# A new instruction order, a warm-up without a gap and a last row stored in unequal parts, in a kernel of four layers on one core

## The chip, the cores and the metric

The kernel runs on one core of a Trainium2 chip. The core has five engines with a queue each: TensorE (PE: matrix products, transposes; its weight loads, PEld, run beside the products), VectorE (DVE), ScalarE (ACT), GpSimd (POOL) and SyncE (SP, which here only issues DMAs). They run side by side and wait for one another by semaphores; within one queue the order is fixed. The metric is the time of one execution on the device in microseconds (us); less is better.

## The reference

Four layers in a row act on one sequence of 2048 rows of 512 numbers (bfloat16), two kinds in turn:

```python
def _A_ref(q, k, v, shift_k, ssm_k, ssm_D):
    k_shift = sum of 4 shifted copies of k, each times a row of shift_k
    kv = k_shift * v
    y = causal convolution of kv with ssm_k along the sequence (by FFT), per column
    y = y + kv * ssm_D
    return q * y

def _B_ref(x, w_gate, w_up, w_down):
    return (silu(x @ w_gate) * (x @ w_up)) @ w_down

x = A_q
x = x + _A_ref(_layernorm(x), A_k, A_v, A_shift_k, A_ssm_k, A_ssm_D)
x = x + _B_ref(_layernorm(x), B_w_gate, B_w_up, B_w_down)
x = x + _A_ref(_layernorm(x), A_k, A_v, A_shift_k, A_ssm_k, A_ssm_D)
x = x + _B_ref(_layernorm(x), B_w_gate, B_w_up, B_w_down)
```

The hidden width of B is 1792. The convolution in A has the same inputs both times and does not depend on x, so its result y is computed once and used in both A layers.

## The kernel before, in words

**The convolution.** The sequence is cut into four blocks of 512 rows. Each block of `kv` (by PE: "shift" products with diagonal matrices `dg`, then a DVE product with `vt`) and each block of the kernel `ssm_k` (called `hn`, turned by PE or DMA into `hs`) is brought into a spectrum by PE products with tables `fwd` of sines (made at the start on DVE and ACT). ACT copies the spectra out of PSUM (`ev`, `X`, `H`), DVE forms sums and differences (`G`, `m`), multiplies spectra (`t`, `Z`), and PE brings the result back with the table `inv` (`Yk`). This work is spread over the first two thirds of the run, beside the feed-forward units.

**The feed-forward units.** Each block of rows is worked in two halves of 256 rows, and in two layers, so there are 16 units. A unit's rows are normalised (DVE or ACT statistics; the power of -1/2 on GpSimd, `rstd`; the scaled rows `n` or `z`), multiplied with `Yk` and added to `xc`, normalised again and turned by a DMA on SP's queue into `zT` (the first unit's by PE). Then PE forms gate and up products in pairs of 128 hidden columns (`pf`, line 311), ACT evacuates them (silu into `sg`, line 970; copy into `ht`, line 974), DVE multiplies `ht` by `sg` (line 977), PE multiplies by the down weights (`pd`, line 990), ACT copies `pd` out (`dn`, line 1034), DVE adds it to the rows (line 1037), and for the second layer SP stores each row tile (line 1045).

**What sets the order.** Every instruction is first recorded with an engine, an assumed cost and its buffers (`add`). Then a written list, `ORDER`, gives each recorded step its place; the steps are put into the engines' queues in that sequence. `Plan.order` works out planned start times from the assumed costs, which decide which of the rotating buffers a tile takes. `Plan.issue` emits the steps, and where the plan leaves PE without work for over 0.5 us before 32 us it puts products of a constant tile in (`warm`, line 1264, called "warm-up products" here; PSUM tile `wm`); how many comes from the planned gap at 0.106 us each. In the kernel before they read a tile `wz` that DVE sets to 0.5.

**The opening.** SP loads `hn`, `kn` (keys), `vt`, `xc`, a second `hn`, `vt`, and the gate weights; two DMAs turn `fwd` into `inv`; then a key block and the other weights follow. ACT's queue loads the four taps (`tapR`) and one row (`drow`), then loads its function table and computes the sines. PE warms up, turns the taps (line 1133), transposes `hn` (line 477) and `kn` (line 366), and starts on the spectra (lines 311 and 458).

**The last row.** The very last unit ends with a row tile of 512 columns that is split into two parts of 256: DVE adds the first part from PSUM to the rows (line 1008) and SP stores it; PE itself adds the rows to the second part (line 949), ACT copies it out (line 1011) and stores it from its own queue (line 1014).

Of the kernel before, what the change touches and what calls it, by code (L numbers as in the profile page):

```python
# [9 lines left out]
P = 128  # L10
# [6 lines left out]
LN_EPS = 1e-5  # L17
# [33 lines left out]
LASTV = True  # L51
ORDER = [
# [186 lines left out]
def kernel(  # L239
# [1024 lines left out]
    def warm(ring, slot, n):  # L1264
        t = psp.tile([P, P], F32, name="wm", tag=f"{ring}{slot}")
        for _ in range(n):
            nc.tensor.matmul(t[:], lhsT=wz.t[:], rhs=wz.t[:], start=True, stop=True)  # L1267
# [33 lines left out]
```

## Time and profile before

| what | value |
|---|---|
| median of 3 runs | 344.79 us (344.21 to 345.18) |
| the profiled execution's own time | 344.93 us |
| its span, first to last instruction | 343.2 us |
| PE busy | 336.4 us (98%) |
| weight loads busy | 248.6 us (72%) |
| DVE busy | 283.4 us (83%) |
| ACT busy | 253.9 us (74%) |
| POOL busy | 35.3 us (10%) |
| gate and up products (line 311), 1792 | 110.4 + 110.2 us, 273 ns each as recorded |
| down products (line 990), 440 | 102.4 us |
| warm-up products, 31 | 3.6 us |
| power steps on GpSimd, 24 + 8 | 690 to 1790 ns each |

The recorded time of a product includes its way through the array and overlaps the next one; the distance between starts is shorter (64 gate and up products in 6.99 us, 109 ns each). Busy shares are therefore shares of time with something running, not of peak. Idle time of an engine that is not the bound costs nothing; the chain of waits tells which engine was the bound at each moment.

### The profile page before, as it was taken

How to read it: one execution, taken by the hardware profiler on the slowest of the kernel's cores; microseconds unless marked ns; L12 is line 12 of the kernel's file. 1: busy time of each engine (PE TensorE's matmuls, PEld its weight loads, DVE VectorE, ACT ScalarE, POOL GpSimd, SP SyncE). 2: the span in 40 equal slices, each digit the busy share in tenths (PEclk: the TensorE clock that was granted, in tenths of full speed). 3: DMA queues.
4: the chain of work that ended last, by engine and by line, in shares of the span. 5: the costliest groups of instructions: out<-in, count | busy, mean ns of one | idle time of the engine just before them, and what ended most of it. 6: DMA issues, size and time to landing. Idle time of an engine off the chain costs nothing.

```text
span 343.2 us, 6553 instructions
## 1 busy us (share of the span) xinstructions
PE 336.4 (98%) x2579; PEld 248.6 (72%) x2610; DVE 283.4 (83%) x482; ACT 253.9 (74%) x504; POOL 35.3 (10%) x46
## 2 busy tenths in 40 slices
PE   8999999999999999999999999999999999999996
PEld 7756868768687676858586777768685877777783
DVE  8899999899999999899999999989998433726022
ACT  6999999899997765958789995779475464446261
POOL 4010100203111000103110100201101001000000
PEclk9999999999999999999999999999999999999999
DMA  7999218310116044040101014210101100110101
GB/s 273 336 316 341 52 27 112 77 32 0 34 31 94 14 95 138 2 94 3 32 2 46 2 46 79 76 32 1 32 0 33 35 13 0 39 39 8 24 26 37
DMA packets 42088, 22.95 MB, mean 67 GB/s; under 512 B 33861, under 2 KB 39882, under 8 KB 42058
## 3 DMA queue, kind: packets, MB, share of 16 engines
q1 hardware_dynamic: 41904, 22.47, 26.6%
q8 instruction: 20, 0.33, 0.4%
q14 instruction: 10, 0.08, 0.1%
q10 hardware_dynamic: 154, 0.07, 0.1%
HBM read 12.33 MB, written 2.10 MB: 42 GB/s over the span
## 4 chain that ended last, share of the span: by engine, by line
PE 91%; ACT 4%; DVE 3%; issue 1%
PE pf L311 54%; PE pd L990 28%; PE ps L311 6%; PE ps L458 1%; ACT H L419 1%; PE wm L1267 1%; DVE bnst L809 1%; ACT hs L487 1%; PE pt L477 1%; ACT X L419 0%; ACT n L859 0%; PE pt L366 0%; DVE m L540 0%; DVE t L665 0%; DVE Z L667 0%
## 5 line engine op out<-in xcount | busy, mean ns | idle before, releaser
L311 PE MATMUL pf<-zT,wu_sb 128*128 128x256 bf16 x896 | 110.4, 273 | 0.1
L311 PE MATMUL pf<-zT,wg_sb 128*128 128x256 bf16 x896 | 110.2, 273 | 0.2
L990 PE MATMUL pd<-wd_sb,ht 128*128 128x512 bf16 (+1 forms) x440 | 102.4, 372 | 1.2
L311 PEld LDWEIGHTS <-wu_sb 128*128 128x128 bf16 x896 | 87.7, 98 | 16.4
L311 PEld LDWEIGHTS <-wg_sb 128*128 128x128 bf16 x896 | 87.6, 98 | 16.5 <-issue 0.8
L974 ACT CAST ht<-pf 128x512 bf16<-128x512 f32 x112 | 64.0, 591 | 29.3 <-PE pf L311 29.1
L970 ACT ACTIVATE sg<-pf 128x512 bf16<-128x512 f32 x112 | 65.5, 603 | 17.4 <-PE pf L311 15.1
L990 PEld LDWEIGHTS <-ht 128*128 128x128 bf16 x462 | 45.2, 98 | 42.5
L977 DVE TENSOR_TENSOR ht<-ht,sg 128x1024 bf16<-128x1024 bf16 (+1 forms) x64 | 39.0, 617 | 24.0 <-ACT sg L970 18.7
L814 POOL TENSOR_TENSOR rstd<-ve,nhalf 128x2 f32<-128x2 f32 x24 | 23.0, 958 | 217.8 <-DVE ve L812 207.6
L1034 ACT CAST dn<-pd 128x512 bf16<-128x512 f32 x30 | 17.0, 589 | 21.0 <-PE pd L990 20.9
L809 DVE BATCH_NORM_STATS2 bnst<-xc 128x6 f32<-128x512 bf16 x48 | 31.6, 684 | 0.6
L419 ACT ACTIVATE X<-ps 128x512 bf16<-128x512 f32 x32 | 19.2, 611 | 4.0 <-PE ps L311 3.4
L653 DVE TENSOR_TENSOR t<-X,G 128x2048 bf16<-128x2048 bf16 x18 | 21.9, 1218 | 0.1
L657 DVE TENSOR_TENSOR t<-X,G 128x2048 bf16<-128x2048 bf16 x18 | 21.9, 1216 | 0.0
L1037 DVE TENSOR_TENSOR xc<-xc,dn 128x1024 bf16<-128x1024 bf16 x15 | 10.3, 689 | 13.4 <-ACT dn L1034 13.2
L665 DVE TENSOR_TENSOR t<-t,t 128x2048 bf16<-128x2048 bf16 x12 | 14.7, 1222 | 0.3
L667 DVE TENSOR_TENSOR Z<-Z,t 128x2048 bf16<-128x2048 bf16 x12 | 14.6, 1220 | 0.2
L840 POOL TENSOR_TENSOR rstd<-ve,nhalf 128x2 f32<-128x2 f32 x8 | 8.7, 1088 | 59.2 <-ACT ve L838 59.1
L419 ACT ACTIVATE H<-ps 128x512 bf16<-128x512 f32 x24 | 13.8, 610 | 0.1
L886 DVE TENSOR_TENSOR n<-n,Yk 128x1024 bf16<-128x1024 bf16 x15 | 10.3, 688 | 4.1 <-ACT n L859 3.8
L604 ACT ACTIVATE kc<-kTb,tapF 128x512 bf16<-128x512 bf16 x16 | 12.1, 783 | 0.0
(105 smaller groups left out, 323.3 us busy)
## 6 DMA issues: line engine op xcount, KB each, us to landing
hn<-in_A_ssm_k_dram SPq DMA_DIRECT2D x4, 512.0 KB, 4.1
vt<-in_A_v_dram SPq DMA_DIRECT2D x4, 512.0 KB, 5.9
xc<-in_A_q_dram SPq DMA_DIRECT2D x4, 512.0 KB, 5.3
out_dram<-xc SPq DMA_DIRECT2D x15, 128.0 KB, 1.8
wg_sb<-in_B_w_gate_dram SPq DMA_DIRECT2D x1, 1792.0 KB
wu_sb<-in_B_w_up_dram SPq DMA_DIRECT2D x1, 1792.0 KB, 8.5
wd_sb<-in_B_w_down_dram SPq DMA_DIRECT2D x1, 1280.0 KB, 12.0
kn<-in_A_k_dram SPq DMA_DIRECT2D x1, 512.0 KB, 4.5
```

What stands on the lines that cost most here:

```text
L311: nc.tensor.matmul(o, lhsT=lhsT, rhs=rhs, start=(n == 0), stop=(n == len(terms) - 1))
L419: add("ACT", act(D), lambda: nc.scalar.activation(out=view(), in_=ps.t[:], func=ACT.Copy, scale=scale), r=[ps], w=[(buf, keys)], conv=conv)
L653: dve(n * D, lambda t1=t1, part=part: nc.vector.tensor_mul(out=t1.t[:], in0=x.t[:, sl, 0, :], in1=g.t[:, sl, part, :]), [(x, key(slots, (0 ...
L657: dve(n * D, lambda t2=t2, part=part: nc.vector.tensor_mul(out=t2.t[:], in0=x.t[:, sl, 1, :], in1=g.t[:, sl, 1 - part, :]), [(x, key(slots ...
L665: dve(n * D, lambda t1=t1, t2=t2, comb=comb: nc.vector.tensor_tensor(out=t1.t[:], in0=t1.t[:], in1=t2.t[:], op=comb), [t2], [t1], conv=conv)
L809: add("DVE", 0.6, lambda st=st, i=i: nc.vector.bn_stats(out=st.t[:], in_=xs[c].t[:, i, :]), r=[(xs[c], (i,))], w=[st])
L814: add("POOL", pw, lambda: nc.gpsimd.tensor_tensor(out=rstd.t[:], in0=ve.t[:], in1=nhalf.t[:].to_broadcast((P, n)), op=ALU.pow), r=[ve, nha ...
L970: add("ACT", act(D), lambda ps=ps, o=o, sg=sg: nc.scalar.activation(out=sg.t[:, o:o + 2, :], in_=ps.t[:], func=ACT.Silu), r=[ps], w=[(sg, ...
L974: add("ACT", act(D), lambda ps=ps, o=o, ht=ht: nc.scalar.copy(out=ht.t[:, o:o + 2, :], in_=ps.t[:]), r=[ps], w=[(ht, (o // 2,))], due=(uni ...
L977: dve(n * W, lambda sg=sg, ht=ht: nc.vector.tensor_mul(out=ht.t[:], in0=ht.t[:], in1=sg.t[:]), [sg], [ht], due=(unit, k / pairs, 0.0, "h"))
L990: nc.tensor.matmul((pds[o] if not cs.start else pds[HP]).t[:, cs], lhsT=ht.t[:, q, o * P:(o + 1) * P], rhs=wt["d"].t[:, ft, cs], start=(ft ...
L1034: add("ACT", act(D), lambda o=o: nc.scalar.copy(out=dn.t[:, o, :], in_=pds[o].t[:]), r=[pds[o]], w=[(dn, (o,))], due=(unit, 1.0, 3.0, "h"))
```

## The change

Five things change in the code.

1. The warm-up products read `ones`, a constant of the framework that GpSimd writes before the engines start on the program, and DVE's memset of `wz` is gone.
2. The count of warm-up products leaves out a margin of 0.3 us where the planned gap starts between 0 and 8 us. The program now has 25 and 8 of them ahead of and behind the tap products (22 and 5 before), and 16 at a later place in the opening (4 before).
3. The last row tile is split into 320 and 192 columns instead of 256 and 256, with assumed costs to match.
4. The list `ORDER` is replaced by another one. The steps are the same; their sequence differs on every engine, from the first microseconds to the end.
5. A switch `VE_D` is added that would move one small step of the statistics from ACT to DVE. It is off, so nothing changes by it.

```diff
@@ -49,65 +49,67 @@
 LASTV = True
+TAIL = 320
+VE_D = False
 ORDER = [
-    0, 8, 122, 2, 4, 5, 12, 9, 3, 6, 1, 31, 32, 33, 10, 14, 7, 11, 15, 16, 18, 21, 17, 20, 22, 23, 36, 30, 56, 73, 153, 24, 40, 25, 41, 34, 42, 38,
...
+    0, 37, 6, 3, 4, 17, 9, 7, 8, 1, 2, 15, 61, 12, 5, 10, 11, 13, 39, 19, 14, 20, 16, 21, 25, 40, 38, 62, 63, 101, 30, 43, 22, 55, 26, 42, 24, 46, 56,
...
@@ -222,7 +224,7 @@
                         if busy.get((ring, i), 0.0) <= t:
-                            n = int((start - max(t, 0.3) - 0.3) / 0.106)
+                            n = int((start - t - (0.0 if 0.0 < t < 8.0 else 0.3)) / 0.106)
                             if n > 0:
                                 warm(ring, i, n)
@@ -835,8 +837,12 @@
-        add("ACT", TINY, lambda: nc.scalar.activation(out=ve.t[:], in_=sm.t[:, n:2 * n], func=ACT.Identity, scale=1.0 / D, bias=eps.t[:]),
-            r=[(sm, range(n, 2 * n)), eps], w=[ve])
+        if VE_D:
...
+        else:
+            add("ACT", TINY, lambda: nc.scalar.activation(out=ve.t[:], in_=sm.t[:, n:2 * n], func=ACT.Identity, scale=1.0 / D, bias=eps.t[:]),
+                r=[(sm, range(n, 2 * n)), eps], w=[ve])
@@ -942,7 +948,7 @@
-                halves = (slice(0, D // 2), slice(D // 2, D)) if unit == LAST_UNIT and o == HP - 1 else (slice(0, D),)
+                halves = (slice(0, TAIL), slice(TAIL, D)) if unit == LAST_UNIT and o == HP - 1 else (slice(0, D),)
@@ -980,7 +986,7 @@
-                halves = (slice(0, D // 2), slice(D // 2, D))
+                halves = (slice(0, TAIL), slice(TAIL, D))
@@ -989,7 +995,7 @@
-                    add("PE", pe(n) if not last else pe(n, D // 2), go, r=[ht, (wt["d"], (0 if fts[0] == 0 else 1,))],
+                    add("PE", pe(n) if not last else pe(n, css[0].stop - css[0].start), go, r=[ht, (wt["d"], (0 if fts[0] == 0 else 1,))],
@@ -1002,13 +1008,13 @@
-            for half_, (eng, cs) in enumerate((("DVE", slice(0, D // 2)), ("ACT", slice(D // 2, D)))):
+            for half_, (eng, cs) in enumerate((("DVE", slice(0, TAIL)), ("ACT", slice(TAIL, D)))):
                 copy = nc.scalar.copy if eng == "ACT" else nc.vector.tensor_copy
                 if LASTV and not half_:
-                    add(eng, 0.35, lambda cs=cs: nc.vector.tensor_add(out=x.t[:, i, cs], in0=x.t[:, i, cs], in1=pds[o].t[:, cs]),
+                    add(eng, 0.42, lambda cs=cs: nc.vector.tensor_add(out=x.t[:, i, cs], in0=x.t[:, i, cs], in1=pds[o].t[:, cs]),
...
@@ -1046,8 +1052,7 @@
-    wz = whole("wz", [P, P])
-    add("DVE", 0.07, lambda: nc.vector.memset(wz.t[:], 0.5), w=[wz], due=-80)
+    ones = nc.const_aps.tensor(1.0, (P, P), BF16)
@@ -1264,7 +1269,7 @@
         for _ in range(n):
-            nc.tensor.matmul(t[:], lhsT=wz.t[:], rhs=wz.t[:], start=True, stop=True)
+            nc.tensor.matmul(t[:], lhsT=ones, rhs=ones, start=True, stop=True)
```

More of the change, by code (lines that the diff above doesn't have):

```diff
@@ L837, in ln_stats_act @@
         ve, rstd = new("ve", "ve", [P, n], F32), new("rs", "rstd", [P, n], F32)
-        add("ACT", TINY, lambda: nc.scalar.activation(out=ve.t[:], in_=sm.t[:, n:2 * n], func=ACT.Identity, scale=1.0 / D, bias=eps.t[:]),
-            r=[(sm, range(n, 2 * n)), eps], w=[ve])
+        if VE_D:
+            add("DVE", 0.08, lambda: nc.vector.tensor_scalar(out=ve.t[:], in0=sm.t[:, n:2 * n], scalar1=1.0 / D, scalar2=LN_EPS,
+                                                             op0=ALU.mult, op1=ALU.add), r=[(sm, range(n, 2 * n))], w=[ve])
+        else:
+            add("ACT", TINY, lambda: nc.scalar.activation(out=ve.t[:], in_=sm.t[:, n:2 * n], func=ACT.Identity, scale=1.0 / D, bias=eps.t[:]),
+                r=[(sm, range(n, 2 * n)), eps], w=[ve])
         add("POOL", PWA, lambda: nc.gpsimd.tensor_tensor(out=rstd.t[:], in0=ve.t[:], in1=nhalf.t[:].to_broadcast((P, n)),
@@ L1004, in ffn @@
                 due=(unit, 1.0, 20.0, None))
-            for half_, (eng, cs) in enumerate((("DVE", slice(0, D // 2)), ("ACT", slice(D // 2, D)))):
+            for half_, (eng, cs) in enumerate((("DVE", slice(0, TAIL)), ("ACT", slice(TAIL, D)))):
                 copy = nc.scalar.copy if eng == "ACT" else nc.vector.tensor_copy
                 if LASTV and not half_:
-                    add(eng, 0.35, lambda cs=cs: nc.vector.tensor_add(out=x.t[:, i, cs], in0=x.t[:, i, cs], in1=pds[o].t[:, cs]),
+                    add(eng, 0.42, lambda cs=cs: nc.vector.tensor_add(out=x.t[:, i, cs], in0=x.t[:, i, cs], in1=pds[o].t[:, cs]),
                         r=[pds[o], (x, (i,))], w=[(x, (R + half_,))], due=(unit, 1.0, 3.0, "h"))
                 else:
-                    add(eng, 0.35, lambda cs=cs, copy=copy, half_=half_: copy(out=x.t[:, i, cs], in_=pds[HP if half_ else o].t[:, cs]),
+                    add(eng, 0.3, lambda cs=cs, copy=copy, half_=half_: copy(out=x.t[:, i, cs], in_=pds[HP if half_ else o].t[:, cs]),
                         r=[pds[HP if half_ else o]], w=[(x, (R + half_,))], due=(unit, 1.0, 3.0, "h"))
```

114 rows, old and new, of the table ORDER are left out of this document.

## The prediction, made before the changed kernel had run

> **What bounds the kernel now.** I read the page first (busy shares, slices), then the chain of waits in order of time, then busy times by stretch, then the timeline of the first 16 us and of the last 12.
>
> ```profile
> PE 336.4 (98%) x2579; PEld 248.6 (72%) x2610; DVE 283.4 (83%) x482; ACT 253.9 (74%) x504; POOL 35.3 (10%) x46
> ```
>
> TensorE (PE) is busy for 98% of the span, so the question is only where the missing 7 us lie and whether the change reaches them. The stretches (length, then busy time of PE, weight loads, DVE, ACT, POOL) answer that:
>
> ```profile
> 12.00:16.00 4.00, 3.95 (x51) 3.06 (x50) 3.63 (x6) 3.44 (x10) 0.00 (x0) 1.00 1.22 339
> 16.00:20.00 4.00, 4.00 (x26) 2.04 (x25) 3.96 (x8) 3.44 (x9) 1.04 (x1) 1.00 1.06 221
> 24.00:28.00 4.00, 3.60 (x41) 2.63 (x40) 3.93 (x9) 4.00 (x9) 0.00 (x0) 1.00 1.06 382
> 28.00:33.60 5.60, 5.20 (x58) 3.51 (x56) 5.30 (x15) 5.60 (x13) 0.69 (x1) 1.00 1.21 359
> 33.60:100.00 66.40, 66.03 (x502) 49.40 (x507) 64.88 (x107) 64.24 (x134) 9.09 (x9) 1.00 0.26 46
> 100.00:200.00 100.00, 99.53 (x747) 73.50 (x753) 96.97 (x145) 77.77 (x152) 10.13 (x9) 1.00 0.22 46
> 200.00:300.00 100.00, 99.53 (x744) 73.46 (x751) 78.26 (x132) 63.37 (x126) 9.33 (x10) 1.00 0.15 33
> 300.00:335.00 35.00, 34.86 (x276) 27.10 (x277) 11.04 (x24) 18.11 (x33) 1.38 (x2) 1.00 0.10 27
> ```
>
> From 33.6 to 335 us PE idles 0.37 + 0.47 + 0.47 + 0.14 = 1.45 us in all. That is the most a better order can win in the feed-forward part. Before 33.6 us the limit is shared: DVE and ACT are full from 20 us on. After 335 us there is the last row and its store. The chain of waits shows the opening (start, duration):
>
> ```profile
> 1.04 2.53 PE wm L1267 x22
> 3.79 0.66 PE wm L1267 x5
> 4.49 1.86 PE pt L477 x16
> 6.35 0.85 PE pt L366 x8
> 9.48 5.08 PE ps L311 x71
> 14.62 4.49 PE ps L458 x20
> ...
> 32.08 0.56 PE ptz L920 x8
> 32.63 1.11 PE ps L311 x17
> ```
>
> PE carries the chain from 4.49 to about 19 us, then ACT, then a short DVE and PE tail into the first gate matmul at 33.6 us. The column of the granted clock says 1.00 throughout, yet PE starts at half speed: eight transposes take 0.85 us here (106 ns each), while 64 products of the same 128 columns later take 3.74 us (58 ns each). The timeline gives the moment of the step:
>
> ```profile
> 7.00 0.52 PE L311 MATMUL ps<-hs,fwd 128*128 128x512 bf16 x1
> 7.36 0.60 PE L311 MATMUL ps<-hs,fwd 128*128 128x512 bf16 x2
> ```
>
> The next product starts 0.36 us later, between the slow 0.427 (4 x 0.1067) and the fast 0.216; so 0.29 us ran slow, and the step lies at 7.0 + 0.29 = 7.29 us. Useful work ran at half speed from 4.49 to 7.29, a loss of 1.4 us on PE.
>
> The profiled execution took 344.93 us: span 343.2 and 1.73 around it. It is 0.14 above the median of the runs (344.79).
>
> **The change, part by part.**
>
> *Warm-up.* Before, the first warm-up product waits for a DVE memset (0.82 to 0.99) and starts at 1.04. Now it reads a constant that GpSimd writes at 0.30, so it starts where the engines are released, about 0.85. There are 25 instead of 22, then the four tap products, then 8 instead of 5. At 0.107 us: 0.85 + 25 x 0.107 = 3.5, the taps take 0.22 (to 3.74, if the taps have landed as they had at 3.50 before), 8 x 0.107 = 0.86, end 4.60. The first useful transpose then starts at 4.6 to 4.65 instead of 4.49: +0.11 to +0.16. With the step still at 7.29, half of that is won back: +0.07. I take +0.07. [...]
>
> *Sixteen warm-up products in mid opening* (four before) after the first inverse products, at about 24 us: 16 x 0.056 = 0.9 us of PE. They lie beside PE's wait for ACT's evacuations: from 24 to 33.6 PE idles 0.40 + 0.40 = 0.8 us, and the four old ones add 0.22. Cost 0; if that cover is gone, 0.9 - 0.22 = 0.7.
>
> *Queues of the first 8 us.* ACT's second load waits for a memset that DVE now runs behind one phase product (ends about 1.7, not 1.25), so the table load behind it starts at 2.0 instead of 1.59 and the sines end at about 4.05 and, with one diagonal between them, 5.1 (4.5 before). DVE negates them behind six diagonals, until 6.2; their first reader is PE at 7 us: hidden, with 0.8 us to spare. Beyond that each us would be a us. On GpSimd the zeroing of the key's margin goes behind the four diagonals (to about 7.0; first reader near 9.7): hidden by 2.7. SP's list is the same up to the last weight load, and the weights that its two table transposes hold up land at 27 us and are read at 34.4: hidden.
>
> *Order of the opening.* PE runs the same 32 transposes, 16 products of the table with the kernel rows and 64 shift products up to about 14.8 us, in another order, so that point moves only with the start. From there ACT must deliver eight evacuations for the DVE products. Between the last "ev" and the eighth X, ACT's list held one squared pass (0.77), two row copies (1.0 each), 0.3 and 0.18: 3.2 us besides X. Now it holds two squared passes, one copy, an H (0.5), 0.3 and two of 0.18: 3.7 us. That is +0.5, of which ACT's idle time from 12 to 20 us (0.56 + 0.56) can take all. DVE then has four Z combinations (0.35 each) instead of three behind the last product: +0.35, part of it run earlier. Bounds: 0 and +0.5; I take +0.2, since DVE was full, not ACT, when the last X came. ACT has one copy fewer (0.51) ahead of the first zT copy; nothing is won, since PE's own 17 products (1.11 us) end at 33.7 anyway.
>
> *Order of the feed-forward part.* The same instructions, so only waits count. Up to 1.45 us could go. I compared, for each of the 16 units, PE's work ahead of its first product with DVE's or ACT's work ahead of its normalised rows. Units 4 and 5 lose 1.3 us of distance each and unit 9 2.2, units 7 and 14 gain 2.0 and 5.2, the other units stay within 1; the second and third inverse gain 1.3 and 3.6, the last loses 2.6 where DVE has a fifth of its time free. The sixth unit changes most. Before:
>
> ```profile
> 119.89 0.41 DVE L864 TENSOR_SCALAR z<-xc,mv,rstd 128x512 bf16<-128x512 bf16 x1
> ```
>
> ```profile
> 128.48 1.19 SPq L893 DMA_TRANSPOSE zT<-z  x1
> ```
>
> ```profile
> 132.43 9.77 PE pf L311 x88
> ```
>
> Now five more DVE operations of 2048 columns and one more of 1024 precede that second z: 5 x 1.2 + 0.65 = 6.65, end 120.30 + 6.65 = 126.95. The transposing DMA takes 2.4 us: 129.35. PE has three "ps" and eight "pd" products fewer ahead: 11 x 0.216 = 2.4, so it comes at 130.0. It still passes, with 0.7 us to spare. The power step on GpSimd varies from 0.69 to 1.79 us, so planning it long costs nothing by itself, and before, no PE wait was behind it but 0.3 us at the opening. Value 0; ends -1.45 and +2.
>
> *Last row.* PE's total is the same; its last two products are 192 columns wide, so the first part ends 2 x 0.083 before the end instead of 2 x 0.109.
>
> ```profile
> 339.78 0.42 DVE L1008 TENSOR_TENSOR xc<-xc,pd 128x256 bf16<-128x256 bf16 x1 [0.40 <-PE pd L990]
> 340.00 0.37 ACT L1011 CAST xc<-pd 128x256 bf16<-128x256 f32 x1 [4.12 <-PE pd L990]
> 340.23 0.33 SPq L1014 DMA_DIRECT2D out_dram<-xc  x1
> 340.40 0.38 ACTq L1014 DMA_DIRECT2D out_dram<-xc  x1
> ```
>
> DVE's add: 0.42 for 256 columns, 0.69 for 512, so 0.49 for 320; it ends at 339.83 + 0.49 = 340.32 and SP issues at 340.35. ACT's copy: 0.37 and 0.59, so 0.32 for 192; its store goes at 340.35 instead of 340.40. The later store is 0.05 earlier: -0.05.
>
> **Sum** on the profiled execution: 0.07 + 0 + 0.2 + 0 - 0.05 = +0.2, that is 345.15; on the median 344.79 + 0.2 = 345.0. Since a start that is not unlucky for the clock lies below 7.29 on average, I shade it to 344.9.
>
> **Rivals.**
> [...]
> B. *The sixth unit waits.* DVE is 97% busy from 100 to 200 us, so a delay there is not made up. From 0.7 us of lateness on, each us is a us. DVE idled 1.5 us between 33.6 and 100; should the new list idle 2 us more, PE waits 1.3, and the neighbouring units 4 and 5, with 0.9 and 1.6 us left by the same working, as much again at worst: 346.2 (up to 347).
> C. *The opening is really shorter.* If ACT takes the +0.5 in its idle time and the wait of 0.3 behind the power step goes, with 0.5 of the 1.45 later on: 344.93 - 0.9 = 344.0, inside the 0.3% band.
> D. *The change of the last row does not show*: 0.05 us is below what can be measured; in itself no other time.
>
> **How the numbers follow.** 0.3% of 344.79 is 1.03 us, about what a measurement of this kernel can tell from no change. Chances: forecast with C and D 0.54 (344.0 to 345.8), A 0.18, B and the uncovered warm-up products 0.28. So faster 0.18, same 0.54, slower 0.28. The range for 8 in 10 reaches into A down to 343.5 and into B up to 346.4.
>
> **What would show it.** [...] The forecast is wrong if the first gate matmul moves by over 1 us, or if PE idles over 2 us behind it.

## The result and the profile after

The changed kernel takes 347.82 us (median of 6 runs, 346.23 to 348.69) against 344.80 us before (6 runs, 344.21 to 345.18). The ratio is 1.0093 with an interval of 1.0078 to 1.0109: slower by 0.9%. The forecast was 344.9 us, with a range that ended at 346.4: the median lies above it. The profiled execution took 347.17 us: span 345.4 and 1.77 around it, against 343.2 and 1.73.

The busy line of the page for the changed kernel, and the stretches from 33.6 to 300 us, the first one cut at the place that matters (length, then busy time of PE, weight loads, DVE, ACT, POOL):

```profile
PE 338.7 (98%) x2628; PEld 249.1 (72%) x2628; DVE 282.1 (82%) x481; ACT 252.2 (73%) x504; POOL 41.0 (12%) x46
```

```profile
33.60:64.00 30.40, 30.40 (x238) 23.03 (x236) 29.13 (x40) 27.14 (x62) 5.36 (x3) 1.00 0.29 63
64.00:66.20 2.20, 0.18 (x2) 0.01 (x1) 0.52 (x1) 2.17 (x5) 0.00 (x0) 1.00 0.00 0
66.20:100.00 33.80, 33.80 (x248) 24.14 (x248) 32.67 (x65) 33.70 (x67) 6.67 (x6) 1.00 0.15 36
100.00:200.00 100.00, 99.92 (x756) 73.73 (x755) 97.11 (x144) 79.14 (x153) 14.14 (x9) 1.00 0.21 46
200.00:300.00 100.00, 100.00 (x762) 74.37 (x760) 79.45 (x134) 62.29 (x127) 8.07 (x10) 1.00 0.14 30
```

PE works from 33.6 to 300 us with one hole of any size (0.08 us are idle elsewhere): from 64.2 to 66.2 it does nothing. The share of busy time, 98% as before, hides that. GpSimd's time (POOL) grew most for its size, 41.0 us against 35.3, for the same power steps. (PE's 338.7 against 336.4 is no such growth: 31 of its records are missing before, see below.) The waits of PE from 33 to 345 us have one entry, 2.0 us long, where the kernel before has none:

```profile
PE pf L313 <- ACT sg L976: 2.0, 1, 2.0
```

The chain of waits of the changed kernel runs through that place (start, duration):

```profile
59.37 0.30 ACT ve L844
59.67 0.07 issue
59.74 3.72 POOL rstd L846
63.46 0.02 issue
63.48 0.30 ACT nmr L858
63.78 0.03 issue
63.81 0.81 ACT n L865
...
65.56 0.58 ACT sg L976
66.14 0.04 issue
66.19 1.90 PE pf L313 x15
```

One power step on GpSimd takes 3.72 us. ACT stands at `nmr`, which reads its result, and then does `nmr`, `n`, `nmr`, `n`; the `sg` that would empty PE's next PSUM tile is queued behind these four. The timeline of DVE and GpSimd shows what the power step waits for. Changed kernel:

```profile
58.82 1.20 DVE L659 TENSOR_TENSOR t<-X,G 128x2048 bf16<-128x2048 bf16 x1
59.94 1.22 DVE L655 TENSOR_TENSOR t<-X,G 128x2048 bf16<-128x2048 bf16 x1
61.08 0.68 DVE L983 TENSOR_TENSOR ht<-ht,sg 128x1024 bf16<-128x1024 bf16 x1
61.68 1.22 DVE L667 TENSOR_TENSOR t<-t,t 128x2048 bf16<-128x2048 bf16 x1
59.74 3.71 POOL L846 TENSOR_TENSOR rstd<-ve,nhalf 128x2 f32<-128x2 f32 x1 [12.69 <-ACT ve L844]
```

The same step of the kernel before:

```profile
58.85 1.22 DVE L657 TENSOR_TENSOR t<-X,G 128x2048 bf16<-128x2048 bf16 x1
59.99 1.22 DVE L653 TENSOR_TENSOR t<-X,G 128x2048 bf16<-128x2048 bf16 x1
61.24 1.23 DVE L665 TENSOR_TENSOR t<-t,t 128x2048 bf16<-128x2048 bf16 x1
59.97 1.79 POOL L840 TENSOR_TENSOR rstd<-ve,nhalf 128x2 f32<-128x2 f32 x1 [12.88 <-ACT ve L838]
```

Before, the sum `t<-t,t` reads the product just ahead of it, so it starts at 61.24, 0.03 us after that product's end (59.99 + 1.22 = 61.21); the power step ends at 61.76, 0.55 after the same end. In the changed kernel the order puts an `ht` product between the two. Now every DVE step starts 0.08 us before the end of the one ahead of it, there is no pause until 62.90, and the power step ends at 63.45, again 0.55 after that.

The other places are as forecast or nearly so. The chain shows the opening:

```profile
0.78 2.83 PE wm L1272 x25
...
4.86 1.70 PE pt L479 x16
6.56 0.67 PE pt L368 x12
```

Sixteen transposes take 1.70 us (106 ns each) and the next twelve 0.67 (56 each), so full speed comes at about 6.56 us (7.29 before). The first gate product starts at 33.71, against 33.74 (by the chain; the timeline, in which the records of products overlap, has 33.55 and 33.58). At the end both last stores are issued in the same moment:

```profile
341.98 0.49 DVE L1014 TENSOR_TENSOR xc<-xc,pd 128x320 bf16<-128x320 bf16 x1 [1.33 <-PE pd L996]
342.14 0.32 ACT L1017 CAST xc<-pd 128x192 bf16<-128x192 f32 x1 [5.03 <-PE pd L996]
342.49 0.39 ACTq L1020 DMA_DIRECT2D out_dram<-xc  x1
342.49 0.33 SPq L1020 DMA_DIRECT2D out_dram<-xc  x1
```

### The profile page after: what moved, and what is told of

Read it like the earlier page. It is cut to its first block, busy times and chain, and to the rows that moved or that the text cites. A ratio compares the mean times of both kernels' runs of the same rounds, so it can differ in the third digit from the quotient of the medians.

```text
span 345.4 us, 6615 instructions
## 1 busy us (share of the span) xinstructions
PE 338.7 (98%) x2628; PEld 249.1 (72%) x2628; DVE 282.1 (82%) x481; ACT 252.2 (73%) x504; POOL 41.0 (12%) x46
## 4 chain that ended last, share of the span: by engine, by line
PE 93%; ACT 3%; POOL 1%; DVE 1%; issue 0%
PE pf L313 54%; PE pd L996 27%; PE ps L313 7%; PE ps L460 2%; PE wm L1272 1%; POOL rstd L846 1%; PE pt L479 1%; ACT sg L976 0%; ACT jk L836 0%; PE ps L799 0%; DVE bnst L811 0%; ACT dn L1040 0%; POOL rstd L816 0%; ACT ht L980 0%; PE pt L368 0%
## 5 line engine op out<-in xcount | busy, mean ns | idle before, releaser
L996 PE MATMUL pd<-wd_sb,ht 128*128 128x512 bf16 (+1 forms) x462 | 105.0, 373 | 0.0
L980 ACT CAST ht<-pf 128x512 bf16<-128x512 f32 x112 | 64.2, 592 | 28.7 <-PE pf L313 28.5
L976 ACT ACTIVATE sg<-pf 128x512 bf16<-128x512 f32 x112 | 66.4, 607 | 22.2 <-PE pf L313 13.0
L816 POOL TENSOR_TENSOR rstd<-ve,nhalf 128x2 f32<-128x2 f32 x24 | 26.4, 1101 | 197.8 <-DVE ve L814 197.8
L846 POOL TENSOR_TENSOR rstd<-ve,nhalf 128x2 f32<-128x2 f32 x8 | 10.9, 1363 | 74.6 <-ACT ve L844 74.6
L421 ACT ACTIVATE H<-ps 128x512 bf16<-128x512 f32 x24 | 14.7, 616 | 0.6 <-PE ps L313 0.5
L606 ACT ACTIVATE ka<-kTb,tapF 128x512 bf16<-128x512 bf16 x16 | 12.6, 803 | 0.0
```

What stands on the lines that cost most here:

```text
L421: add("ACT", act(D), lambda: nc.scalar.activation(out=view(), in_=ps.t[:], func=ACT.Copy, scale=scale), r=[ps], w=[(buf, keys)], conv=conv)
L816: add("POOL", pw, lambda: nc.gpsimd.tensor_tensor(out=rstd.t[:], in0=ve.t[:], in1=nhalf.t[:].to_broadcast((P, n)), op=ALU.pow), r=[ve, nha ...
L976: add("ACT", act(D), lambda ps=ps, o=o, sg=sg: nc.scalar.activation(out=sg.t[:, o:o + 2, :], in_=ps.t[:], func=ACT.Silu), r=[ps], w=[(sg, ...
L980: add("ACT", act(D), lambda ps=ps, o=o, ht=ht: nc.scalar.copy(out=ht.t[:, o:o + 2, :], in_=ps.t[:]), r=[ps], w=[(ht, (o // 2,))], due=(uni ...
L996: nc.tensor.matmul((pds[o] if not cs.start else pds[HP]).t[:, cs], lhsT=ht.t[:, q, o * P:(o + 1) * P], rhs=wt["d"].t[:, ft, cs], start=(ft ...
```

## The experiments

The theory: DVE keeps GpSimd out of its power step as long as DVE's products follow one another without a pause; ACT's fixed order hands the delay on to PE. Its rivals: the long power step is a side effect of something else that holds PE; or one of the other parts of the change (warm-up, last row) costs the time. Where an experiment adds copies or products on DVE, nothing reads what they write (or it is what was there already), and the output is the same.

Profiled executions of one and the same opening reached the first gate product anywhere from 32.8 to 35.2 us (see the last section). So for a single profile I also give the time from the first gate product as the timeline has it to the end of the span: 343.2 - 33.58 = 309.62 us before and 345.4 - 33.55 = 311.85 us after, +2.23.

### Which part costs the time

Three kernels do one part of the change each, from the kernel before.

```diff
 # order alone: the new list, with wz's memset kept as its first step
-ORDER = [0, 8, 122, 2, 4, 5, ...
+ORDER = [0, 1, 38, 7, 4, 5, ...
```

> The kernel before with the new list of orders alone; the warm-up products read the old tile in the old counts, the last row stays 256 and 256. Theory P (the wait behind the power step is the whole loss): all of it comes with the order, so a power step of 3.7 us near 60 us, a PE wait of about 2.0 us near 66 us, and a ratio of 1.006 to 1.010. Rival W (the new warm-up or the new last row costs as well): ratio at most 1.005.

Measured 347.62 us (346.53 to 349.72), ratio 1.0103 [1.0078, 1.0128]. The power step takes 3.72 us, and PE's list of waits has the entry again:

```profile
PE pf L309 <- ACT sg L968: 2.0, 1, 2.0
```

```diff
 # warm-up alone: the constant, and the count
-    wz = whole("wz", [P, P])
...
+    ones = nc.const_aps.tensor(1.0, (P, P), BF16)
...
-n = int((start - max(t, 0.3) - 0.3) / 0.106)
+n = int((start - t - (0.0 if 0.0 < t < 8.0 else 0.3)) / 0.106)
```

> The kernel before with the warm-up on the constant ones and the new count (25 and 8 products) alone. Prediction's term: first useful transpose 0.1 to 0.2 us later (4.6 to 4.7), the step to full speed near where it fell before on average: ratio 0.9995 to 1.0005. [...]

Measured 344.09 us, ratio 0.9999 [0.9990, 1.0009]: nothing.

```diff
 # last row alone
-slice(0, D // 2), slice(D // 2, D)
+slice(0, 320), slice(320, D)
```

> The kernel before with the last row split into 320 and 192 columns alone. Prediction's term: the later of the two last stores is issued 0.05 us earlier, nothing else moves: ratio 0.9995 to 1.0003, not told apart from 1.

Measured 344.54 us, ratio 1.0011 [1.0002, 1.0021]: 0.1 to 0.7 us slower, where the working gave 0.05 faster. The order alone gives a ratio of 1.0103, the whole change 1.0093: within these intervals the order is the whole of the loss.

### A pause in DVE's list

The changed kernel, with a copy of one column to the neighbouring column and back again behind the first `t` product; the second copy reads what the first wrote.

```diff
             o.emit()
+            if o.n in PAUSE:      # PAUSE = {299}, the t product of line 659
+                pause()
...
+    def pause():
+        nc.vector.tensor_copy(out=tick[:, 1:2], in_=tick[:, 0:1])
+        nc.vector.tensor_copy(out=tick[:, 0:1], in_=tick[:, 1:2])
```

> The changed kernel with two one-column copies on DVE, the second reading the first, right behind the t product that runs when the power step at 59.74 us is issued. Theory P (pause): a power step on GpSimd gets through only where DVE really stops between two steps, and it ends about 0.55 us after that; ACT's queue stands behind it. Then the step lasts about 0.9 us instead of 3.71, the 2.0 us wait of PE before 66.19 us goes, and the kernel falls from about 1.009 to 1.000 to 1.002 of the kernel before. Theory A (ACT's list): the silu evacuations stand behind too much other ACT work in the new order, whatever GpSimd does: the power step may be shorter but PE still waits 1.5 us or more there, ratio 1.007 to 1.010. Theory C (clock): the loss is in the lower granted clock of the executions (0.994 to 0.998), not in this wait: ratio near 1.005 or above and the clock still below 1.

```profile
59.03 0.84 POOL L849 TENSOR_TENSOR rstd<-ve,nhalf 128x2 f32<-128x2 f32 x1 [12.68 <-ACT ve L847]
58.11 1.21 DVE L662 TENSOR_TENSOR t<-X,G 128x2048 bf16<-128x2048 bf16 x1
59.24 0.15 DVE L1280 COPY tick<-tick 128x1 f32<-128x1 f32 x1
59.42 0.15 DVE L1281 COPY tick<-tick 128x1 f32<-128x1 f32 x1
```

The power step takes 0.84 us, PE's wait is gone, and the kernel takes 344.30 us (343.91 to 345.13), ratio 0.9986 [0.9967, 1.0004]. DVE was given more work, and 3.5 us came off the median (347.82 against 344.30), 2.3 us in the profiles from the first gate product to the end (311.85 against 309.57). The step ends at 59.87, which is 0.55 after the end of the product (59.32), not after the first copy. So I left the second copy out:

> The changed kernel with only one one-column copy on DVE at the place where the run with two was tried, so that nothing there reads the result of the step just before it. Theory P: without that dependence DVE does not stop, the power step stays at 3.7 to 3.9 us, PE's wait at about 2.0 us, ratio 1.006 to 1.010. Rival G (any short or narrow DVE step lets GpSimd in): the power step lasts about 0.9 us and the ratio is 0.998 to 1.001, as with two copies.

```profile
60.26 1.21 DVE L662 TENSOR_TENSOR t<-X,G 128x2048 bf16<-128x2048 bf16 x1
61.18 0.84 POOL L849 TENSOR_TENSOR rstd<-ve,nhalf 128x2 f32<-128x2 f32 x1 [12.68 <-ACT ve L847]
61.38 0.15 DVE L1280 COPY tick<-tick 128x1 f32<-128x1 f32 x1
```

344.64 us, ratio 1.0004 [0.9984, 1.0025], power step again 0.84. The copy starts before the product ahead of it ends (60.26 + 1.21 = 61.47), so there is no pause at all; my condition "a step that reads the one before it" was too narrow. Here a step that reads only one tensor let GpSimd in as well.

### Moving the pause

First, the changed kernel with two steps swapped, so that the `ht` product comes ahead of the second `t` product and the sum again follows the product that it reads.

```diff
 # places in ORDER of steps 298 (t, line 655) and 377 (ht, line 983)
-    298 at 374, 377 at 375
+    377 at 374, 298 at 375
```

> The changed kernel with two DVE steps exchanged in the order: the ht product goes ahead of the second t product, so that the sum t<-t,t reads the result of the step just before it. No step is added. Theory P: DVE's next real stop moves from 62.90 to about 61.76 us, the power step lasts about 2.6 us instead of 3.71, PE's wait falls from 2.0 to about 0.9 us: ratio about 1.005. Theory A: PE's wait and the ratio stay as they are (1.009).

```profile
59.31 2.57 POOL L844 TENSOR_TENSOR rstd<-ve,nhalf 128x2 f32<-128x2 f32 x1 [12.69 <-ACT ve L842]
61.37 1.23 DVE L665 TENSOR_TENSOR t<-t,t 128x2048 bf16<-128x2048 bf16 x1
```

345.79 us, ratio 1.0031 [1.0012, 1.0050], where about 1.005 was expected; power step 2.57, PE's wait 0.9, as expected. No step was added: two steps changed places, the first pause, of 0.04 us, came 1.1 us sooner after the power step's start, and 1.1 us of power step and 1.1 of PE's wait went.

Then the other way round: the kernel before, with one product of 256 columns that reads nothing of its neighbours, put between the product and the sum (so that the pause closes), and, as a control, put behind the sum.

```diff
+    def pause():
+        nc.vector.tensor_tensor(out=pad[:], in0=wt['g'].t[:, 0, 0:256], in1=wt['g'].t[:, 1, 0:256], op=ALU.mult)
```

> The kernel before with one independent DVE product of 256 columns put between the second t product and the sum that reads it, at the power step of 59.97 us. It closes the stop at 61.2 us. Theory P: the power step lasts until DVE has to wait for the normalised rows, about 63.4 us, so about 3.5 us instead of 1.79; ACT's normalisation and what is behind it come 1.8 us later and PE waits 0.3 to 1.5 us: ratio 1.001 to 1.004. Theory A: the power step stays near 1.8 us, ratio 1.000.

> The control to the run before: the same independent DVE product in the kernel before, but behind the sum, so that the stop at 61.2 us stays. Theories P and A: the power step lasts about 1.8 us as before and the time is that of the kernel before within 0.3 us (ratio 0.999 to 1.001).

Between (the first fence, with PE's entry), then behind:

```profile
60.22 3.13 POOL L843 TENSOR_TENSOR rstd<-ve,nhalf 128x2 f32<-128x2 f32 x1 [12.88 <-ACT ve L841]
61.39 0.28 DVE L1275 TENSOR_TENSOR pad<-wg_sb 128x256 bf16<-128x256 bf16 x1
61.59 1.22 DVE L668 TENSOR_TENSOR t<-t,t 128x2048 bf16<-128x2048 bf16 x1
```

```profile
PE pf L314 <- ACT ht L977: 1.3, 1, 1.3
```

```profile
61.64 1.80 POOL L843 TENSOR_TENSOR rstd<-ve,nhalf 128x2 f32<-128x2 f32 x1 [12.87 <-ACT ve L841]
```

Between: 346.30 us, ratio 1.0032 [1.0013, 1.0052]. Behind: 344.92 us, 1.0003 [0.9982, 1.0024]. The same 0.2 us of DVE work costs over a microsecond in one place and nothing in the other. The 3.13 is less than the 3.5 expected: the step ended 0.55 after the sum's end (62.81), where a `bn_stats` began, which reads one tensor.

### Taking the handover away

The changed kernel, with the four ACT steps that read the power step's result planned behind the two `sg` and the `H` that stood behind them. The power step is left as it is.

```diff
 # ACT's list
-nmr, n, nmr, n, sg, H, sg
+sg, H, sg, nmr, n, nmr, n
```

> The changed kernel with the four ACT steps that read the power step's result (the two nmr and the two n near 63.5 us) planned behind the two sg and the H that stood behind them; the power step and DVE's steps around it are left as they are. If the changed kernel's PE wait is handed on by ACT's order (ACT stands at nmr until the power step is done, and the sg that frees PE's tile is queued behind it), the power step stays at about 3.7 us, ACT still waits at nmr until about 63.5 us, and the PE wait of 2.0 us is gone (under 0.2 us): span 345.4 - 2.0 = 343.4 us, time 345.1 us or a little less (344.3 with the one-column copies), ratio 0.999 to 1.002. If PE waited for something else that the long power step or DVE's steps hold back, the PE wait stays near 2 us and the ratio near 1.009.

```profile
61.36 3.71 POOL L844 TENSOR_TENSOR rstd<-ve,nhalf 128x2 f32<-128x2 f32 x1 [12.69 <-ACT ve L842]
```

```profile
67.31 0.69 DVE L890 TENSOR_TENSOR n<-n,Yk 128x1024 bf16<-128x1024 bf16 x1 [2.80 <-ACT n L863]
```

```profile
71.35 1.67 PE L994 MATMUL pd<-wd_sb,ht 128*128 128x512 bf16 x7 [1.21 <-DVE ht L981]
```

Half of this came as expected: the power step still takes 3.71, and the wait for `sg` is gone. But the time is 348.65 us, ratio 1.0111 [1.0075, 1.0147], and the time from the first gate product to the end is 311.84 us, as in the changed kernel. The delay took the other road. DVE, too, has a fixed order, stands 2.80 us at `n<-n,Yk`, and the `ht` products behind it come late, so that PE waits 1.21 and 0.31 us for them and 0.28 for an `ht` copy. So ACT's order is how the delay reached PE first, not why it could not be absorbed.

### More work on DVE

Two kernels were to lengthen DVE's run without a pause by 1.0 and 1.14 us, the second by issuing one `t` product twice.

```diff
 # first: behind the ht product of line 983, three times
+            nc.vector.tensor_tensor(out=jk.t[:], in0=wt['g'].t[:, 0, 0:512], in1=wt['g'].t[:, 1, 0:512], op=ALU.mult)
 # second
+            if o.n in TWICE:      # TWICE = {298}, the t product of line 655
+                o.emit()
```

> The changed kernel with three products of 512 columns on DVE (into a buffer that nothing reads any more) between the product of ht and the last product of the t's near 61.7 us, which keep DVE busy without a pause for about 1.0 us more. If GpSimd's power step gets in only when DVE pauses or has a short step, it ends 1.0 us later (about 4.7 us long) and the PE wait grows from 2.0 to about 3.0 us; if it gets in at one of the new boundaries, it ends earlier by up to 1 us. On the mean granted clock, which was 0.994 to 0.995 in half of the executions of the changed kernel and of the new order alone, and 0.998 to 1.000 in the others: if PE's idle stretch is what lowers it, the longer one lowers it in all or nearly all executions, the windows behind the wait show a granted clock below 1, and the time is 347.2 + 1.0 + about 1.7 = 350 us, ratio 1.015 to 1.018. If the idle stretch has nothing to do with it, about half of the executions show it and the median is near 349 us.

> The changed kernel with the second t product near 60 us (2,048 columns, 1.14 us from start to start) issued twice, so that DVE's run without a pause is 1.14 us longer; the second writes what the first wrote. At the two boundaries between such products the changed kernel's power step did not get in. If it gets in only at a pause, a narrow step or a lucky boundary, it now ends at about +1.14 us, so lasts 4.85 us, the PE wait grows from 2.0 to 3.1 us, and the stretch from the first gate product to the end of the span from 311.85 to 313.0 us: time 348.3 to 349.0 us, ratio 1.012 to 1.016. If the power step gets in at the new boundary, the wait is at most 2 us and the ratio at most 1.009. On the clock: PE waits of 1.3 us and less (six kernels here) never showed a mean clock under 0.998, the one of 2.0 us showed 0.994 to 0.995 in 6 of 12 executions. If PE's idle stretch lowers it, 3.1 us lowers it in most executions, and those take 1.5 to 2 us more (median near 350 us, ratio 1.017 to 1.02); if it has nothing to do with the idle stretch, few or none of these executions show it.

Both got faster than the changed kernel. The first took 346.92 us, ratio 1.0055 [1.0029, 1.0081] (its interval still touches that of the changed kernel), PE's wait 1.2 us; the second 345.44 us, ratio 1.0037 [1.0023, 1.0052]. The power step of the first, then the timeline of the second:

```profile
60.87 2.90 POOL L849 TENSOR_TENSOR rstd<-ve,nhalf 128x2 f32<-128x2 f32 x1 [12.70 <-ACT ve L847]
```

```profile
59.08 1.98 POOL L849 TENSOR_TENSOR rstd<-ve,nhalf 128x2 f32<-128x2 f32 x1 [12.68 <-ACT ve L847]
59.29 1.22 DVE L658 TENSOR_TENSOR t<-X,G 128x2048 bf16<-128x2048 bf16 x1
60.55 1.22 DVE L658 TENSOR_TENSOR t<-X,G 128x2048 bf16<-128x2048 bf16 x1
```

A step that writes the tile of the step before it waits for it as well: the second product starts at 60.55, 0.04 after the first one's end (60.51), and the power step ends at 61.06, which is 60.51 + 0.55. The three products into one buffer did the same (step end 63.77 = 63.22 + 0.55, the first one's end). So what I took for a longer run was a run with pauses in it; 1.14 us more DVE work, with a pause of 0.04, saves about 2 us (ratio 1.0037 against 1.0093). PE's wait for `sg` is gone; 0.6 us of waiting for an `ht` product is left.

### A version that beats both?

The changed kernel with the one copy, and with the last row split in 256 and 256.

```diff
-TAIL = 320
+TAIL = 256
+PAUSE = {299}      # one copy of one column, as above
```

> The changed kernel with the single one-column copy behind the first t product, and the last row split in 256 and 256 as before. The wait of 2.0 us is gone; outside of it the new order had about 0.3 us fewer PE waits than the old one, and the old split of the last row was 0.3 to 0.4 us faster in the run of that part alone. So 344.7 - 0.3 - 0.1 = 344.3 us beside a before of 344.7 us, ratio 0.9975 to 1.0000; if the short pauses were chance, or the old row brings nothing in this order, 1.0005.

345.01 us (343.59 to 345.84), ratio 1.0009 [0.9992, 1.0025]: the loss is repaired and nothing is won that these runs could tell.

## Why the prediction was wrong

| kernel | power step | PE's wait for `sg` (where named, for `ht`) | first gate product to end |
|---|---|---|---|
| before | 1.79 | 0 | 309.62 |
| changed | 3.71 | 2.0 | 311.85 |
| order alone | 3.72 | 2.0 | 311.71 |
| ACT steps behind | 3.71 | 1.8 (`ht`) | 311.84 |
| three products | 2.90 | 1.2 | 310.94 |
| pause closed in the kernel before | 3.13 | 1.3 (`ht`) | 310.76 |
| steps swapped | 2.57 | 0.9 | 310.79 |
| `t` product twice | 1.98 | 0.6 (`ht`) | 310.30 |
| two copies | 0.84 | 0 | 309.57 |
| one copy | 0.84 | 0 | 309.31 |
| one copy, old last row | 0.83 | 0 | 309.22 |

**The step that failed** is the order of the feed-forward part: "The power step on GpSimd varies from 0.69 to 1.79 us, so planning it long costs nothing by itself, and before, no PE wait was behind it but 0.3 us at the opening. Value 0; ends -1.45 and +2." The last column rises with PE's wait, and the wait for `sg` is the power step less 1.68 us (3.71 - 1.68 = 2.03, 2.90 - 1.68 = 1.22, 2.57 - 1.68 = 0.89). Against the three kernels with a copy (309.37 on average) the new order's other rows rise by 0.3 to 0.7 us more than the wait; the runs do not show why. The term was +2.0, the upper end, and not 0, and PE idled over 2 us behind its first gate product, which the prediction had named as the sign of being wrong. The wait does not account for all of the result: the profiled executions differ by 2.2 us (347.17 against 344.93), the medians by 3.0, because three of the six executions took 348.3 to 348.7 us. No profile shows one of those, so that part stays open (last section). Two things in the profile of before could have told it. The longest power step there, 1.79, was no property of that step: un-hindered ones take 0.69, so the longer ones had waited, and the timeline shows for what. And the new list could be held against that: which DVE steps stand beside each power step, and does any of them wait for its neighbour? I compared distances between units, in DVE work and PE work, which is blind to an engine that stands still beside a busy one. That "no PE wait was behind it" only said that 1.79 us was covered; the run with the closed pause shows that 1.34 us more (3.13 against 1.79) cost PE 1.3, so that almost no cover was left.

**The gain to be had** was overrated. I read 1.45 us of PE idle time between 33.6 and 335 us. The busy line of before has 2579 products but 2610 weight loads, that of the changed kernel 2628 of each, though its program has only 3 + 3 + 12 = 18 products more; so 31 products were missing from the record before, and a missing record looks like idle time. The control (the same product behind the sum) has the old order and all 2610 products. Its stretches, the first from 36 us on:

```profile
36.00:100.00 64.00, 63.99 (x487) 47.42 (x486) 62.69 (x104) 61.79 (x130) 9.10 (x9) 1.00 0.22 45
100.00:200.00 100.00, 99.71 (x750) 73.08 (x749) 97.10 (x146) 77.47 (x150) 10.13 (x9) 1.00 0.23 47
200.00:300.00 100.00, 100.00 (x761) 74.30 (x760) 78.83 (x133) 64.16 (x128) 9.31 (x10) 1.00 0.14 30
```

PE idles 0.30 us in them, and 0.29 of that is one wait behind `zT` at 134 us, which the kernel before does not have. So there was next to nothing to win. The four kernels with the old order and no PE wait over 0.3 us (before, control, warm-up alone, last row alone: 309.62, 309.85, 309.90, 309.91) and the three with the new order and a copy (309.57, 309.31, 309.22) differ by their means, 309.82 - 309.37 = 0.45 us. With so little idle time in the old order this cannot be waiting that the new order saves; what it is, the runs do not show.

**Opening**: forecast +0.07 and +0.2, measured 33.71 - 33.74 = -0.03. The first transpose came at 4.86, not 4.60 to 4.65, and the step to full speed at 6.56, not 7.29; the two cancel: +0.37 and -(7.29 - 6.56)/2 = -0.37. That is luck. In other profiles with the same warm-up the sixteen transposes took between 1.08 us (`t` product twice) and 1.86 us (one copy), so full speed comes earlier or later from one execution to the next, and the first gate product came at 32.83 to 35.16 us (last section). Neither the term of +0.07 nor that of +0.2 can be read from one pair of profiles. The sum was shaded from 345.0 to 344.9 because the step was taken to lie below 7.29 us on average; no run shows that average. The profiles of before and after have the step at 7.29 and 6.56, and where the sixteen transposes take 1.08 us it came about 0.4 us behind the start of the first (an estimate: 3.7 of them at 106 ns and 12.3 at 56 make 1.08). The warm-up alone gave 0.9999; the sixteen products in mid opening are not in it (it has four of them there) but in the order alone, and what they cost (0 or 0.7) cannot be read apart from the rest.

**Last row**: the 0.05 us at the issue is there, the durations were right (0.49 and 0.32), but the end of the span does not follow. From the later of the two stores to the end it is 2.57 to 2.80 us in the six profiles with the old split (mean 2.72) and 2.82 to 3.11 in the eight with the new one (mean 2.89). The list makes a difference too: with the old order it is 2.74 to 2.80 for the old split and 3.11 for the new one, with the new order 2.57 and 2.62 against 2.82 to 2.91. So, like with like, the end comes about 0.3 us later after stores that were issued in the same moment, and the term is about +0.25 instead of -0.05. Why is not shown.

**Rivals**: A and C did not come. A, an earlier step to full speed with a time down to 343.5 us, was given a chance of 0.18: the step came 0.73 us earlier (6.56 against 7.29) and the time rose, and the warm-up alone gave 0.9999. B named the right side and nearly the right price (346.2, up to 347), but the wrong place: from 100 to 200 us PE is busy for 99.92 of 100, and nothing waits behind `zT` (three other kernels with the new list, order alone, two copies and ACT steps behind, wait 0.18 to 0.25 us for it at 170 to 175 us). Its argument, that a late step on a full DVE is not made up, held at 64 us.

## What to carry to other kernels

When the order of a tuned kernel is changed, look at each short GpSimd step and at what DVE runs beside it: not at how much, but at whether any step there pauses (because it reads or overwrites the result of the step before; here it started 0.03 to 0.04 us after that one's end) or reads one tensor only. Here the power step got in at all of 127 pauses, and at 34 of 39 steps that read one tensor. Then follow the waiter's own queue on every engine, since what stands behind it is late too, and moving it out of the way on one engine can hand the delay on by another (311.84 us from the first gate product to the end with ACT's steps behind, 311.85 without). An added instruction that makes a pause at the right place can be worth more than its cost: here a second `t` product of 1.22 us, with a pause of 0.04, took 1.55 us off that stretch (311.85 against 310.30).

## What the runs showed of the hardware

GpSimd's power step (two fp32 tensors in SBUF, 128 x 2) takes 0.69 us by itself. If DVE is in a product of two bf16 tensors when it is issued, it ends 0.55 us after the end of such a product, but not always of the first. I counted over the 14 profiles, from 33 us on, for power steps over 0.75 us, the ends of DVE products of two tensors that fall into a step up to 0.5 us before its end (many places recur from kernel to kernel). "Got in" means that the step ended 0.55 us later:

| behind the product | power step got in |
|---|---|
| the next step starts 0.02 us or more after its end | 127 of 127 |
| the next step starts before its end and reads one tensor (copy, statistics, scaling) | 34 of 39 |
| the next step starts before its end (once 0.005 us after it) and reads two tensors | 61 of 139 |

The five misses of the second row are one place in five kernels, where a power step follows another on GpSimd without a gap; it ended 0.68 us after the product. The changed kernel met three of the last kind in a row and lost at each. What decides there is open. Beside such products a power step lasted 3.71 us, and 0.69 without. Between overlapping products GpSimd often did not get in at the end of one (78 of 139 times), so that in the changed kernel it was kept out for 3.2 us, over four products (62.90 - 59.74). What holds it is not shown: the traces give the start and the end of each step alone.

The opening varies by itself: the first gate product came at 33.58, 33.84, 35.25, 32.70 and 33.49 us in the five profiles with the old order, and at 33.55, 33.79, 32.83, 33.11, 34.99, 35.16, 34.66, 34.28 and 32.90 in the nine with the new one. In two of them PE waited 1.3 us for the keys (`kn`). That is more than most terms of the forecast, and a difference of 0.45 us between two orders would hardly show beside it.

Three of the six executions of the changed kernel, and three of the six with its order alone, had a mean granted clock of 0.994 or 0.995 and took 347.9 to 349.7 us; the others had 0.998 to 1.000 and took 346.2 to 347.3. Of the kernels with a PE wait of 1.3 us or less none had a value under 0.998 in their own executions, the kernel before once. I supposed that the stop of 2 us lets the clock fall in some executions. The two runs that were to lengthen the stop shortened it, so this stays open; no profile here shows such an execution.
